# Re-costed transposes and selects in a list scheduler that orders a fused attention and two-mixture kernel

## The chip, the cores and the metric

One core of a Trainium2 chip runs the whole program in one launch. The metric is device time in microseconds, from the program's start to its end on that core. The profiled execution gives, beside its own time, the span from its first to its last instruction.

The engines are TensorE (PE in the rows; PEld is its weight loads), VectorE (DVE), ScalarE (ACT), GpSimd (POOL) and SyncE (SP, which here issues every DMA and every DMA transpose).

## The reference

```python
scores = scale * np.matmul(q, k.transpose(0, 1, 3, 2))
cum = np.cumsum(np.log(np.clip(f, 0.0001, 1.0)), axis=-1)
decay = cum[:, :, :, None] - cum[:, :, None, :]
scores = np.where(causal, -1000000000.0, scores + decay)
attn = softmax(scores)                       # over the last axis
x = np.matmul(attn, v)                       # 4 batches, 8 heads, 576 rows, head size 64
x = x.transpose(0, 2, 1, 3).reshape(2304, 512)
h = x @ w_in                                 # 512 -> 2048
x = np.maximum(0.01 * h, h) @ w_out          # 2048 -> 512
g = x @ w_gate                               # 512 -> 1536
out = (silu(g) * (x @ w_val)) @ w_out2       # 1536 -> 512
```

Everything is float32 outside; the weights arrive as 64-bit words from which the kernel assembles float32 by integer operations.

## The kernel before, in words

**Precision.** Most products run as three half-precision products of a high and a low half (TERMS = high x high, high x low, low x high). `split` makes the two halves: ScalarE writes the high half, VectorE the low one from it.

**Units of work.** Each batch is cut into two units of queries, the first of 320 (three tiles of 128, the first half empty) and the second of 256 (two tiles). For a unit, `attention` goes through four pairs of heads. For every head it loads queries and keys (`in_qk_dram`), makes TensorE's score products, lets VectorE add the causal mask and take the row extreme (the custom instruction that writes `att_bytes` from a bank), lets ScalarE take the exponential, and `probs` writes the two halves of the normalised probabilities into one tile. A DMA transpose on SyncE turns that tile: 12 blocks of 128 x 128 two-byte numbers in a first unit, 18 in a second one. There are 56 of these. `pv` (a product of transposed probabilities and values) then fills the rows of one pair, and a ScalarE and a VectorE instruction write its high and low half into `xs_buf`, which lies in `moe_bytes`. The first unit of the first batch goes another way, in float32, with diagonal matrices that GpSimd makes by `affine_select` (line 858).

**The mixture behind.** While the attention of one unit runs, TensorE gets the first mixture of the unit before as filling: `moe_h` (banks from `moe_bytes` and `wi_bytes`) and `moe_y` (banks from `g_bytes` and `wo_bytes`). So at the end of every unit there is a handover: the last `pv` of the unit, its two halves, and then the first `moe_h` group, which reads them. Between them VectorE also assembles the next weights from words (tiles `stage`, `wi_bytes`, `wo_bytes`) and stores them for later. After the last unit the second mixture runs alone, on TensorE above all, to the end.

**What sets the order.** No instruction is issued when its function is called. `Plan.record` keeps it with a reckoned duration from `cost` (line 149 on), `link` finds what depends on what, and `emit` (line 382) searches an order. `schedule` is a list scheduler over five queues: at each step the engine that is free first takes the ready piece that is due earliest. `backward` sets new due times from the far end, and the next round uses them. This is done in rounds, for two lead times of loads. `trial` then reckons each order's end under several cases of random lateness of the DMAs, and the order with the smallest sum is issued, in program order on each engine. On the chip every engine works through its own queue strictly in that order and waits by semaphores where a piece's input is not there. The reckoned durations are thus in the order only; they are no part of the program.

In the first 18 us, and where the plan has TensorE pause early on, `emit` puts warming matmuls on a spare bank (line 412).

Since all instructions are issued from line 415, rows are told apart by tiles, not by lines.

## Time and profile before

| | us |
|---|---|
| median of 3 runs | 925.02 |
| lowest and highest | 922.46, 925.94 |
| the profiled execution, its own time | 925.66 |
| its span, first to last instruction | 923.9 |

The profile's rows say how long an engine was busy, how long one instruction took on average, and in brackets how long the engine stood before it and who ended that. A waiting engine costs time only if it is on the way to the end.

### The profile page before, as it was taken

The page shows a single profiled execution, that of the slowest core. Times are in us where ns is not written, and L with a number is a line of the kernel's source. Part 1 is how long each engine was busy: PE and PEld are TensorE (multiplying, and loading weights), DVE is VectorE, ACT ScalarE, POOL GpSimd, SP SyncE. Part 2 cuts the span into 40 slices and gives each one's busy share as a digit, 9 for nine tenths or more (in the row PEclk, how much of TensorE's full clock was granted, in tenths as well). Part 3 has the DMA queues.
Part 4 walks back from the last instruction along what each step waited for, and adds up shares of the span by engine and source line. Part 5 has one row for each costly group of instructions (what it writes and reads, how often), then busy time and mean ns, then how long its engine had stood idle before and what let it go on. Part 6 is the DMA issues. An engine that isn't in the chain of part 4 may idle for free.

```text
span 923.9 us, 25387 instructions
## 1 busy us (share of the span) xinstructions
PE 908.8 (98%) x10018; PEld 776.7 (84%) x10018; DVE 794.1 (86%) x2078; ACT 676.1 (73%) x1665; POOL 45.4 (5%) x119
## 2 busy tenths in 40 slices
PE   9999999999999999899999999999999999999998
PEld 5666678877688777788778899999999999999997
DVE  7999999988899999799788999986778695968685
ACT  8886689988689887688886878774647474755553
POOL 3410000000000010000000000000000000000000
PEclk9999999999999999999999999999999999999999
DMA  7568985797999999989867452110101000100001
GB/s 229 179 202 217 271 212 115 187 248 172 259 270 259 255 263 229 298 249 254 188 147 191 140 178 96 64 59 20 37 18 31 25 25 25 37 25 2 26 6 42
DMA packets 163431, 132.81 MB, mean 144 GB/s; under 512 B 117432, under 2 KB 130752, under 8 KB 163280
## 3 DMA queue, kind: packets, MB, share of 16 engines
q1 hardware_dynamic: 163312, 131.20, 53.5%
q8 instruction: 78, 1.28, 0.6%
q14 instruction: 41, 0.34, 0.1%
HBM read 79.99 MB, written 22.83 MB: 111 GB/s over the span
## 4 chain that ended last, share of the span: by engine, by line
PE 58%; DVE 7%; DMA 3%; ACT 3%; issue 1%; POOL 0%; SPq 0%; ACTq 0%; DVEq 0%; POOLq 0%
PE bank L415 58%; DVE att_bytes L415 2%; DVE stage L415 1%; DVE wo_bytes L415 1%; ACT att_bytes L415 1%; DMA tb<-out_dram 1%; ACT moe_bytes L415 1%; DMA att_bytes<-att_bytes 1%; DVE smalls L415 1%; DVE wi_bytes L415 1%; DMA att_bytes<-in_qk_dram 1%; DMA gate_val_dram<-wo_bytes 1%; DVE g_bytes L415 1%; DVE tb L415 0%; DVE ta L415 0%
## 5 line engine op out<-in xcount | busy, mean ns | idle before, releaser
L415 PEld LDWEIGHTS <-att_bytes 128*128 128x128 f16 (+1 forms) x4062 | 233.8, 100 | 18.3 <-issue 14.7
L415 PEld LDWEIGHTS <-wi_bytes 128*128 128x128 f16 x2292 | 192.2, 98 | 42.4 <-issue 3.1
L415 PE MATMUL bank<-g_bytes,wo_bytes 128*128 128x256 f16 (+2 forms) x1472 | 209.7, 299 | 0.0
L415 PE MATMUL bank<-moe_bytes,wi_bytes 128*128 128x320 f16 (+1 forms) x1536 | 194.5, 286 | 1.5 <-ACT moe_bytes L415 1.5
L415 ACT ACTIVATE att_bytes<-att_bytes,smalls 128x320 f32<-128x320 f32 (+11 forms) x308 | 173.7, 591 | 30.1 <-DVE smalls L415 25.5
L415 PEld LDWEIGHTS <-wo_bytes 128*128 128x128 f16 x1344 | 128.1, 98 | 33.5 <-issue 1.8
L415 DVE TENSOR_TENSOR wi_bytes<-bank,wi_bytes 128x256 f32<-128x256 f32 x270 | 109.4, 418 | 45.0 <-PE bank L415 43.6
L415 PEld LDWEIGHTS <-g_bytes 128*128 128x128 f16 x1620 | 125.9, 98 | 9.0
L415 ACT ACTIVATE wi_bytes<-wi_bytes,smalls 128x256 f32<-128x256 f32 (+2 forms) x129 | 69.9, 555 | 44.9 <-DVE wi_bytes L415 42.4
L415 PE MATMUL bank<-wi_bytes,att_bytes 128*128 128x128 f16 x1680 | 98.7, 219 | 0.5 <-ACT wi_bytes L415 0.3
L415 DVE SCALAR_TENSOR_TENSOR att_bytes<-att_bytes,smalls 128x576 f16<-128x576 f32 (+5 forms) x148 | 86.8, 614 | 4.1 <-ACT att_bytes L415 3.7
L415 PE MATMUL bank<-stage,att_bytes 128*128 128x128 f16 (+1 forms) x1389 | 86.7, 221 | 0.6 <-DVE wi_bytes L415 0.6
L415 ACT COPY wi_bytes<-bank 128x256 f32<-128x256 f32 x108 | 38.4, 363 | 51.8 <-PE bank L415 47.6
L415 DVE CUSTOM_DVE_ANT_0 att_bytes<-bank,att_bytes 128x320 f32<-128x320 f32 (+5 forms) x160 | 67.7, 441 | 7.2 <-PE bank L415 7.1
L415 POOL PARTITION_ALL_REDUCE smalls<-smalls x54 | 28.2, 523 | 757.1 <-DVE smalls L415 718.3
L415 PE MATMUL bank<-att_bytes 128*64 128x256 f16 (+4 forms) x828 | 55.5, 262 | 5.5 <-DMA att_bytes<-att_bytes 5.2
L415 ACT ACTIVATE wi_bytes<-wo_bytes 128x256 bf16<-128x256 f32 x108 | 44.0, 410 | 19.2 <-DVE wo_bytes L415 19.2
L415 PE MATMUL bank<-wo_bytes,g_bytes 128*128 128x256 f16 x432 | 55.0, 273 | 0.0
L415 DVE TENSOR_TENSOR g_bytes<-moe_bytes,g_bytes 128x320 f16<-128x320 f32 (+1 forms) x80 | 44.6, 564 | 8.2 <-ACT g_bytes L415 7.8
L415 PE MATMUL bank<-tb 68*128 68x256 f32 (+3 forms) x144 | 49.9, 360 | 1.7 <-ACT att_bytes L415 1.1
L415 DVE SCALAR_TENSOR_TENSOR stage<-stage 128x512 int32<-128x512 int32 x68 | 46.5, 684 | 0.2
L415 DVE SCALAR_TENSOR_TENSOR wo_bytes<-wi_bytes,smalls 128x512 f32<-128x512 f32 x54 | 40.1, 743 | 6.3 <-ACT wi_bytes L415 6.3
(123 smaller groups left out, 1380.1 us busy)
## 6 DMA issues: line engine op xcount, KB each, us to landing
stage<-in_moe_w_out_dram SPq DMA_DIRECT2D x28, 512.0 KB
att_bytes<-in_qk_dram SPq DMA_DIRECT2D x24, 416.0 KB
stage<-in_moe_w_in_dram SPq DMA_DIRECT2D x16, 512.0 KB
att_bytes<-in_qk_dram SPq DMA_DIRECT2D x24, 320.0 KB
stage<-in_moe_w_gate_dram SPq DMA_DIRECT2D x12, 512.0 KB
stage<-in_moe_w_val_dram SPq DMA_DIRECT2D x12, 512.0 KB
stage<-gate_val_dram SPq DMA_DIRECT2D x12, 512.0 KB
ta<-y_dram SPq DMA_DIRECT2D x18, 256.0 KB
```

What stands on the lines that cost most here:

```text
L415: fn(*args, **kw)
```

## The change

Four numbers of the scheduler's reckoning and the size of its search:

```diff
--- before.py
+++ after.py
@@ -160,7 +160,7 @@
         if eng == "SP":
             k = n(o) * o.shape[0] * mybir.dt.size(o.dtype)
             if method == "dma_start_transpose":
-                return 18.5 * k / 4096, k
+                return 24.4 * k / 4096, k
             return 510.0, k
         m = max(n(x) for x in outs + ins)
         psum = any(x.space == PSUM for x in ins)
@@ -172,7 +172,7 @@
                 return 374.0, 0
             if method == "memset":
                 return 0.83 * m + 48, 0
-            return (4.2 if ptrs else 0.75 if method == "affine_select" else 2.104) * m + 148, 0
+            return (4.2 if ptrs else (3.04 if ins[0].dtype == F32 else 0.75) if method == "affine_select" else 2.104) * m + 148, 0
         if method == "reciprocal":
             return 6.4 * m + 69, 0
         if method == "memset":
@@ -304,7 +304,7 @@
                 d += min(d, max(0.0, COLD - t) / 2)
             free[e] = t + d
             if e == "SP":
-                dma = max(dma, t + 500.0) + op.bytes / (260.0 if op.dur > 1e3 else 280.0)
+                dma = max(dma, t + 500.0) + op.bytes / (210.0 if op.dur > 1e3 else 280.0)
                 op.end = max(dma + 1200.0 + self.MARGIN, t + self.flight(op))
             else:
                 op.end = t + d
@@ -366,7 +366,7 @@
             d = op.dur
             if e == "SP":
                 free[e] = t + d
-                dma = max(dma, t + 500.0) + op.bytes / (260.0 if d > 1e3 else 280.0)
+                dma = max(dma, t + 500.0) + op.bytes / (210.0 if d > 1e3 else 280.0)
                 end[op.idx] = max(dma + 1200.0, t + self.flight(op) - self.MARGIN) + lag[op.idx]
                 continue
             if e == "PE":
@@ -379,7 +379,7 @@
             free[e] = end[op.idx] = t + d
         return max(end)
 
-    def emit(self, rounds=40, trials=4):
+    def emit(self, rounds=60, trials=6):
         self.link()
         bank = self.filler[0].tensor.name
         lags = []
```

`k` is a transpose's bytes, so the first number is nanoseconds per 4,096 bytes that a transpose holds SyncE's queue. The 210 and 260 are bytes per nanosecond in the queue of transfers, for transposes alone (only they are reckoned above 1,000 ns on SyncE). The 3.04 is nanoseconds per column of a float `affine_select` without per-row pointers. With 60 rounds and two lead times 120 orders are made, and each is tried in six cases.

No instruction changes; there are two more warming matmuls (46 in place of 44), and the others stand in another order. On TensorE 398 of the 1,402 scheduled pieces stand elsewhere, on VectorE 1,210 of 1,886, on ScalarE 748 of 1,308, on SyncE 235 of 423, on GpSimd 29 of 115. TensorE's last 653 pieces, VectorE's last 458 and ScalarE's last 332 stand as before.

SyncE's queue at the end of the attention of batch 2, second unit: the last two transposes of the unit, before:

```order
L415 DMA tb_87<-cum_dram 4x640
L415 DMA att_bytes<-in_v_dram 128x640
L415 DMA_TRANSPOSE att_bytes<-att_bytes 128x18x128
L415 DMA stage<-in_moe_w_out_dram 128x1024
L415 DMA att_bytes<-in_qk_dram 128x640
L415 DMA out_dram<-wi_bytes 128x512
L415 DMA att_bytes<-in_qk_dram 128x640
L415 DMA_TRANSPOSE att_bytes<-att_bytes 128x18x128
```

and now:

```order
L415 DMA tb_87<-cum_dram 4x640
L415 DMA att_bytes<-in_v_dram 128x640
L415 DMA_TRANSPOSE att_bytes<-att_bytes 128x18x128
L415 DMA out_dram<-wo_bytes 128x512
L415 DMA stage<-in_moe_w_out_dram 128x1024
L415 DMA att_bytes<-in_qk_dram 128x640
L415 DMA_TRANSPOSE att_bytes<-att_bytes 128x18x128
L415 DMA out_sums_dram<-stage 128x1024
```

A store (`out_dram<-wo_bytes`) and a load (`stage<-in_moe_w_out_dram`) that followed the second transpose now stand between the two, and a load and a store that stood between them now stand ahead of the first.

VectorE at the handover behind batch 0's second unit. The row that writes `moe_bytes` 128x256 is the low half which the next `moe_h` reads; `bank_70` and `bank_71` are score banks, `wo_bytes<-wo_bytes` are low halves of weights. Before:

```order
L415 ISA att_bytes,smalls<-bank_71,att_bytes 128x320
L415 ISA smalls 128x1
L415 TENSOR_SCALAR smalls<-smalls 128x3
L415 RECIPROCAL smalls<-smalls 128x1
L415 TENSOR_TENSOR ta_85<-att_bytes,ta_85 64x320
L415 RECIPROCAL smalls<-smalls 128x3
L415 TENSOR_TENSOR tb_87<-att_bytes,ta_85 64x320
L415 SCALAR_TENSOR_TENSOR wo_bytes<-wo_bytes,smalls 128x512
L415 SCALAR_TENSOR_TENSOR moe_bytes<-bank_72,smalls,moe_bytes 128x256
L415 TENSOR_REDUCE smalls<-att_bytes 128x1
```

and now:

```order
L415 TENSOR_SCALAR smalls<-smalls 128x1
L415 RECIPROCAL smalls<-smalls 128x1
L415 RECIPROCAL smalls<-smalls 128x3
L415 TENSOR_SCALAR smalls<-smalls 128x1 x2
L415 RECIPROCAL smalls<-smalls 128x1
L415 SCALAR_TENSOR_TENSOR wo_bytes<-wo_bytes,smalls 128x512
L415 TENSOR_SCALAR smalls<-smalls 128x3
L415 RECIPROCAL smalls<-smalls 128x3
L415 TENSOR_TENSOR ta_85<-att_bytes,ta_85 64x320
L415 TENSOR_TENSOR tb_87<-att_bytes,ta_85 64x320
L415 SCALAR_TENSOR_TENSOR wo_bytes<-wo_bytes,smalls 128x512
L415 SCALAR_TENSOR_TENSOR moe_bytes<-bank_72,smalls,moe_bytes 128x256
```

Ten instructions that followed the low half now stand ahead of it (one reduction and one weight half of them just above the piece shown); 4.04 us by their own durations in the trace.

VectorE at the handover behind batch 3's first unit, from the last score reduction of that stretch (`bank_71`, 128x288) to the low half (`moe_bytes`, 128x320). Before:

```order
L415 ISA att_bytes,smalls<-bank_71,att_bytes,smalls 128x288
L415 ISA smalls 128x1
L415 SCALAR_TENSOR_TENSOR att_bytes<-att_bytes,smalls 128x448
L415 TENSOR_SCALAR stage<-stage 128x512
L415 SCALAR_TENSOR_TENSOR stage<-stage 128x512
L415 TENSOR_SCALAR smalls<-smalls 128x2
L415 SCALAR_TENSOR_TENSOR moe_bytes<-bank_72,smalls,moe_bytes 128x320
L415 RECIPROCAL smalls<-smalls 128x2
```

and now:

```order
L415 ISA att_bytes,smalls<-bank_71,att_bytes,smalls 128x288
L415 ISA smalls 128x1
L415 RECIPROCAL smalls<-smalls 128x2
L415 SCALAR_TENSOR_TENSOR stage<-stage 128x512
L415 SCALAR_TENSOR_TENSOR wo_bytes<-stage 128x512
L415 SCALAR_TENSOR_TENSOR att_bytes<-att_bytes,smalls 128x576
L415 SCALAR_TENSOR_TENSOR att_bytes<-att_bytes,smalls 128x448
L415 TENSOR_SCALAR smalls<-smalls 128x2
L415 RECIPROCAL smalls<-smalls 128x2
L415 TENSOR_TENSOR tb_87<-att_bytes,ta_85 64x576
L415 SCALAR_TENSOR_TENSOR att_bytes<-att_bytes,smalls 128x576
L415 SCALAR_TENSOR_TENSOR moe_bytes<-bank_72,smalls,moe_bytes 128x320
```

Four instructions stood between the reduction and the low half (the second row writes the reduction's result out); now nine do. Three low halves of probabilities are among them (`att_bytes<-att_bytes,smalls`), a score operand (`tb_87`), two weight assemblies, and the small steps that end in the second reciprocal.

## Rows read from the trace of the kernel before

**Rows 1.** The page's head and busy times by engine.

```profile
span 923.9 us, 25387 instructions
...
PE 908.8 (98%) x10018; PEld 776.7 (84%) x10018; DVE 794.1 (86%) x2078; ACT 676.1 (73%) x1665; POOL 45.4 (5%) x119
```

**Rows 2.** Stretches: bounds and length, busy us by engine, clock, DMA share, GB/s.

```profile
125.00:150.00 25.00, 25.00 (x233) 21.42 (x232) 23.01 (x71) 24.23 (x59) 2.01 (x9) 1.00 0.70 158
350.00:400.00 50.00, 47.65 (x437) 38.57 (x434) 43.53 (x125) 37.77 (x92) 1.30 (x7) 0.97 1.01 268
400.00:450.00 50.00, 48.74 (x446) 40.28 (x446) 48.47 (x145) 44.69 (x116) 0.30 (x2) 1.00 1.00 247
600.00:650.00 50.00, 50.00 (x710) 47.74 (x708) 38.54 (x83) 29.29 (x74) 1.34 (x2) 1.00 0.13 40
```

**Rows 3.** Who waited for whom: total us, times, longest us.

```profile
PE bank L415 <- DMA att_bytes<-att_bytes: 5.2, 3, 2.3
...
PE bank L415 <- ACT moe_bytes L415: 1.5, 3, 0.7
...
PE bank L415 <- ACT att_bytes L415: 1.1, 1, 1.1
```

**Rows 4.** A stretch of TensorE alone: busy us, clock, DMA share, GB/s.

```profile
375.00:385.00 10.00, 10.00 (x89) 0.83 1.00 299
```

**Rows 5.** Timeline near 250 us, SyncE and TensorE: start, us, instruction [idle before, releaser].

```profile
244.99 1.64 SPq L415 DMA_DIRECT2D y_dram<-moe_bytes  x1
...
247.22 3.29 SPq L415 DMA_TRANSPOSE att_bytes<-att_bytes  x1
...
252.31 1.56 PE L415 MATMUL bank<-att_bytes 128*64 128x256 f16 x29 [1.62 <-DMA att_bytes<-att_bytes]
...
254.69 0.50 PE L415 MATMUL bank<-moe_bytes,wi_bytes 128*128 128x256 f16 x3
```

**Rows 6.** Timeline near 110 us, SyncE and TensorE.

```profile
102.15 5.50 SPq L415 DMA_TRANSPOSE att_bytes<-att_bytes  x1
...
110.64 1.53 PE L415 MATMUL bank<-att_bytes 128*64 128x256 f16 x28 [1.26 <-DMA att_bytes<-att_bytes]
```

**Rows 7.** Timeline near 370 us, all engines, some rows left out.

```profile
367.68 4.80 SPq L415 DMA_TRANSPOSE att_bytes<-att_bytes  x1
367.74 0.68 ACT L415 ACTIVATE stage<-wo_bytes 128x512 f32<-128x512 f32 x1 [2.50 <-DVE wo_bytes L415]
...
374.68 1.79 PE L415 MATMUL bank<-att_bytes 128*64 128x256 f16 x29 [2.35 <-DMA att_bytes<-att_bytes]
...
376.40 3.19 PE L415 MATMUL bank<-g_bytes,wo_bytes 128*128 128x320 f16 x12
```

**Rows 8.** SyncE's transposes: count, ns min/median/max, first and last start.

```profile
L415 SPq DMA_TRANSPOSE att_bytes<-att_bytes x56: 1279/3174/7080, 79.0 to 486.9; - x56
```

**Rows 9.** Groups on GpSimd: count, busy us, mean ns, idle before and releasers.

```profile
L415 POOL TENSOR_SCALAR_AFFINE_SELECT g_bytes<-smalls 128x128 f32<-128x128 f32 x24 | 11.5, 506 | 19.6 <-DVE smalls L415 16.8 <-PE bank L412 1.4 <-PE bank L415 1.4
```

**Rows 10.** Groups on TensorE: the warming matmuls.

```profile
L412 PE MATMUL bank<-att_bytes 128*128 128x512 bf16 x44 | 14.0, 456 | 1.6 <-POOL att_bytes L415 1.6
```

**Rows 11.** Timeline near 132 us: VectorE's low half, TensorE's matmuls that read it.

```profile
132.60 0.47 DVE L415 SCALAR_TENSOR_TENSOR moe_bytes<-bank,smalls,moe_bytes 128x256 f16<-128x256 f32 x1
...
132.68 4.54 PE L415 MATMUL bank<-moe_bytes,wi_bytes 128*128 128x256 f16 x40
```

**Rows 12.** Timeline near 434 us: VectorE, ScalarE's high half, TensorE's matmuls that read it.

```profile
431.63 0.17 DVE L415 RECIPROCAL smalls<-smalls 128x2 f32<-128x2 f32 x1
...
433.51 0.51 DVE L415 CUSTOM_DVE_ANT_0 att_bytes<-bank,att_bytes,smalls 128x288 f32<-128x288 f32 x1
...
435.19 0.51 ACT L415 ACTIVATE moe_bytes<-bank,smalls 128x320 f16<-128x320 f32 x1
...
435.75 4.45 PE L415 MATMUL bank<-moe_bytes,wi_bytes 128*128 128x320 f16 x31 [0.71 <-ACT moe_bytes L415]
...
436.24 0.15 DVE L415 RECIPROCAL smalls<-smalls 128x2 f32<-128x2 f32 x1
```

## The prediction

> **What bounds the kernel now.** I read the busy shares first, then who waited for whom, then stretches, then short timelines. TensorE is busy for 908.8 of 923.9 us [rows 1]. So a better order can win only the time in which TensorE pauses, about 15 us, and part of that is the start and the last microseconds. The matmuls stay the same whatever the order.
>
> The second thing to see is that VectorE (DVE) is almost as full in the first half and not in the second: 23.01 of 25 us busy at 125 to 150, 43.53 of 50 at 350 to 400, 48.47 of 50 at 400 to 450, but 38.54 of 50 at 600 to 650 [rows 2]. The two engines are in balance up to about 550 us; behind that TensorE alone decides. And behind that the new order is nearly the old one: of TensorE's 1,402 scheduled pieces the last 653 stand exactly where they stood, as do VectorE's last 458 (the two programs' orders tell this). Everything below therefore plays before about 575 us.
>
> The table of waits names the pauses that the changed numbers are about: TensorE waited three times for a transpose, 5.2 us in all, 2.3 us at most [rows 3]. The last one was costlier than it looks. In the stretch from 375 to 385 us the granted clock averages 0.83 [rows 4]: after the 2.35 us pause TensorE ran at the lower of its two levels for about 10 x (1 - 0.83) / 0.5 = 3.4 us and so lost another 1.7 us. Behind the 1.62 us pause at 252 us [rows 5] the matmuls kept their speed.
>
> **What the new numbers say, against the trace.** A large transpose (18 blocks, 589,824 bytes by its shape) was reckoned to hold SyncE 144 x 18.5 ns = 2.66 us, and is now reckoned at 144 x 24.4 ns = 3.51 us. The three before the pauses held it 5.50, 3.29 and 4.80 us [rows 6, 5, 7], so the new number is nearer. A small one (12 blocks) goes from 1.78 to 2.34 us, while the shortest of all 56 took 1.28 us [rows 8]; for these it moves away from the shortest. A select on a float tile goes from 244 to 537 ns, and the mean is 506 [rows 9]. So two of the three corrections are right. None of them changes an instruction's real cost; they change only the order. The larger search (60 rounds and six cases in place of 40 and four) costs the chip nothing.
>
> On the rate: 589,824 bytes used 252.31 - 247.22 = 5.09 us after issue is 116 GB/s from issue to use [rows 5], and that includes latency, so the trace alone does not tell 260 from 210. The Trainium skill (DMA: Bandwidth & Descriptors, section Latency and other measured facts) gives 261 GB/s for a transpose with a strided middle dimension, close to the old figure and against the new one. By that page the new order would allow 2,809 - 2,260 ns = 0.55 us too much for each large transpose, an estimate, and the slower rival below would gain weight.
>
> **The change part by part.** I use durations of the rows and count what stands ahead of what in the two orders.
>
> 1. Start: 46 warming matmuls instead of 44. The 44 keep TensorE 14.0 us [rows 10], 0.32 us each: **+0.6 us** if both lie on the path, nothing if they fill a real pause. The selects' new order moves GpSimd's instructions by three places at most; I set that at nothing, as GpSimd's 24 selects are 11.5 us in all [rows 9] and lie beside VectorE work.
>
> 2. The product of attention and values at 110 us waits 1.26 us for a transpose issued at 102.15 [rows 6]. In the new order VectorE's last step before that transpose stands where it was, and TensorE has 0.64 us more matmuls ahead of the product (by the same matmuls' spacing in the trace): **-0.6 us**.
>
> 3. The same at 250 us, 1.62 us [rows 5]. The transpose went out at 247.22 because SyncE stood behind a store that held it 1.64 us and was issued ahead of it. The new order puts that store behind the transpose, and three score products ahead of the waiting product; in the trace they lie between its end, 252.31 + 1.56, and 254.69, some 0.8 us. 1.64 + 0.8 is more than 1.62: **-1.6 us**.
>
> 4. The same at 372 us, 2.35 us [rows 7]. Here TensorE gets 2.65 us more ahead of the product (three score products, 1.0 us by their spacing, and one group of 12 matmuls, which at the lower clock took 3.19 us and at the upper one about half). Against that, a load and a store that followed the transpose in SyncE's queue now stand ahead of it. The load needs a buffer whose last reader, ScalarE's 0.68 us step, started at 367.74, so the transpose cannot go before about 368.5 + 2 x 0.4 = 369.3, that is 1.6 us later. The pause shrinks by 2.65 - 1.6 = 1.05 to 1.3 us. That is shorter than the 1.62 after which the clock stayed up, so the 1.7 us go as well: **-2.7 us**. Bounds: 0 and -4.05.
>
> 5. Handover at 130 us, from the last product of one unit to the first hidden-layer matmuls of the mixture that consumes it. ScalarE writes the high half, VectorE the low half (start 132.60, 0.47 us), and the matmuls need the low half four matmuls after 132.68, at 133.1 [rows 11]. It was just in time. In the new order 4.04 us of other VectorE work is moved ahead of it, ten instructions that overlap by some 0.07 us each, so 3.4 us (the order shown above has them). If VectorE is no earlier at that place than now, TensorE pauses 3.4 us; if it has found all of it in gaps, nothing. With 23.01 of 25 us busy I take the upper part: **+2.5 us**.
>
> 6. Handover at 434 us [rows 12]. TensorE stands 0.71 us for the high half. In the new order ScalarE makes that half behind another probability step, and this needs a reciprocal that VectorE does only after seven instructions behind its last score reduction (the first is the 0.17 us reciprocal, the last the 0.15 us one; all seven 3.35 us, less overlap 2.9). From the reduction's end at 434.02 this gives 436.9, then 0.78 and 0.51 us on ScalarE with a step of 0.1 between: 438.3, against 435.7 now, **0 to +2.6 us**. VectorE has 6.5 us of idle time at 350 to 400 [rows 2], which work moved ahead can fill, so I take **+1.5 us**, without a fall of the clock.
>
> Handovers at 186, 254, 308 and 378 us show the same pattern, 1.2 to 6.6 us of VectorE work moved ahead; TensorE gets up to 1 us more there and, at 378, ScalarE and VectorE stood idle for over a microsecond each. I set them at nothing; at the upper end they are in the slower rival.
>
> Sum: 0.6 - 0.6 - 1.6 - 2.7 + 2.5 + 1.5 = **-0.3 us**. The profiled execution took 925.66 us, so 925.4; it lies 0.6 us above the median of 925.02. On the median's footing I say **924.7 us**.
>
> **The rivals.**
> *Faster: the moved work finds real gaps.* If VectorE does the work moved ahead while it would have idled, points 5 and 6 cost nothing, and the sum is -4.3 us. If TensorE's waits for ScalarE go too, 1.5 and 1.1 us [rows 3], it is -6.9: 918.1 us. For it: two of three corrections fit the rows. Against it: VectorE's idle time before 130 us is small.
> *Slower: the handovers pause longer than 2.35 us.* Both late halves then also bring the clock down, as the 2.35 us pause did. Its price is 3.4 + 1.7 at 130 us and 2.6 + 1.7 at 434; with 0.6 at the start, -0.6 and -1.6 from points 2 and 3 and nothing from point 4, that is +7.8: 932.8 us; with a microsecond at each of two more handovers, 934.8. It decides once a half lands more than 2.35 us behind the matmul that needs it. For it: the moved work is in the same direction at every handover. Against it: a pause early in the half makes TensorE late for all that follows and hides later ones.
> *The change does nothing that counts:* the order moves but pauses only change places, since TensorE is full and the later half the same. That gives 925.0, give or take 2, inside my forecast.
>
> **How the numbers follow.** A run of this kernel can tell about 0.5%, 4.6 us, from no change. I give the forecast (with the third rival, some 0.15 of it) 0.50, the faster rival 0.25, the slower 0.25. The range reaches to both rivals' ends, 918 to 935. The forecast's own range is 920.5 to 929.5.
>
> **What would show it.** Right: the wait for transposes falls from 5.2 to about 2 us; no stretch near 375 us has a clock under 1.00; TensorE newly waits 1 to 3 us for VectorE or ScalarE near 133 and 436 us; TensorE's busy time beyond 600 us is unchanged. Wrong: handovers without a pause (then the faster rival), or stretches near 133 or 436 us with a clock under 1.00 (the slower one), or a transpose wait that is as long elsewhere.

## The result and the profile after the change

The change takes 928.97 us (median of 7 runs, 927.92 to 932.79) against 922.46 us for the kernel before (7 runs, 921.74 to 925.94). The ratio is 1.0067, with a 95% interval of 1.0047 to 1.0088: **0.67% slower**, 6.5 us. I had forecast no change (924.7 us) and given slower a chance of one in four. The time lies inside the range, but that is partly luck: the base of the forecast, 925.02 us from three runs, was itself 2.6 us above the later median of before.

The profiled execution took 929.61 us. The page's head, as in [rows 1]:

```profile
span 927.9 us, 25394 instructions
...
PE 909.1 (98%) x10016; PEld 778.5 (84%) x10020; DVE 794.3 (86%) x2078; ACT 677.3 (73%) x1665; POOL 48.4 (5%) x119
```

TensorE, VectorE and ScalarE have hardly more to do. TensorE is busy for 909.1 us as against 908.8, and the span is 4.0 us longer; the difference is TensorE standing still. Who it waited for, as in [rows 3] (total us, times, longest):

```profile
PE bank L415 <- ACT moe_bytes L415: 5.6, 4, 2.4
PE bank L415 <- DMA att_bytes<-att_bytes: 3.4, 2, 2.9
...
PE bank L415 <- DVE wi_bytes L415: 1.6, 3, 0.9
PE bank L415 <- DVE smalls L415: 1.5, 3, 0.7
```

The waits for transposes fell from 5.2 to 3.4 us, but the longest grew from 2.3 to 2.9. The waits for `moe_bytes`, the high halves at the handovers, rose from 1.5 to 5.6 us. The stretches, as in [rows 2, 4] (bounds and length, busy us of PE, PEld, DVE, ACT, POOL, clock, DMA share, GB/s):

```profile
125.00:150.00 25.00, 22.11 (x194) 18.86 (x194) 23.56 (x69) 24.73 (x61) 1.89 (x5) 0.93 0.67 149
131.00:141.00 10.00, 9.85 (x90) 9.00 (x90) 9.47 (x24) 10.00 (x25) 0.32 (x3) 0.83 0.58 149
350.00:400.00 50.00, 47.86 (x446) 38.64 (x444) 46.26 (x137) 38.78 (x95) 1.68 (x8) 1.00 1.04 280
400.00:450.00 50.00, 47.03 (x420) 38.44 (x418) 47.26 (x143) 42.73 (x108) 0.66 (x3) 0.97 0.95 256
436.00:446.00 10.00, 8.21 (x47) 5.26 (x47) 9.46 (x26) 8.13 (x20) 0.00 (x0) 0.83 0.93 217
```

The lower clock that stood at 375 to 385 us in the profiled execution of before is gone (1.00 over 350 to 400). It stands behind 131 and behind 436 us instead, each time 10 x (1 - 0.83) / 0.5 = 3.4 us at 1.2 instead of 2.4 GHz, which costs half of that.

**The handover near 131 us**, timeline (start, us, instruction [idle before, releaser]):

```profile
122.19 0.88 DVE L415 SCALAR_TENSOR_TENSOR att_bytes<-att_bytes,smalls 128x640 f16<-128x640 f32 x1
123.15 1.32 DVE L415 SCALAR_TENSOR_TENSOR att_bytes<-att_bytes,smalls 128x576 f16<-128x576 f32 x2
124.53 3.27 SPq L415 DMA_TRANSPOSE att_bytes<-att_bytes  x1
127.97 0.30 PE L415 MATMUL bank<-att_bytes 128*64 128x256 f16 x1
131.15 2.24 PE L415 MATMUL bank<-att_bytes 128*64 128x256 f16 x29 [2.89 <-DMA att_bytes<-att_bytes]
```

The unit's last product (x1, then x29) starts one matmul at 127.97 and stands 2.89 us for the transpose that SyncE issued at 124.53. That issue came right behind VectorE's two low halves of 576 columns (end 124.47), and ahead of these the change put a low half of 640 columns. But before, the same transpose went out hardly earlier, as SyncE was still held by the one ahead of it, and its product didn't wait:

```profile
124.29 2.74 SPq L415 DMA_TRANSPOSE att_bytes<-att_bytes  x1
...
129.73 1.59 PE L415 MATMUL bank<-att_bytes 128*64 128x256 f16 x30
```

In old_again (below) the issue came at 124.62, later than now, and there was no wait either. So two other things changed. TensorE comes 1.76 us earlier (127.97 against 129.73). And the transpose takes longer: of the 16 signals by which the trace shows it done, the last came 4.6 us after the issue before (128.87) and 6.6 us after it now (131.11). The DMA view of 116 to 133 us, in 40 slices of 0.425 us, shows a stop inside it (7, 5 and 10 GB/s, from 128.75 to 130.03):

```profile
GB/s 288 416 277 136 255 239 173 288 201 139 229 345 230 273 267 237 234 121 139 265 349 386 302 257 134 34 201 214 240 196 7 5 10 212 411 277 390 377 380 386
```

Why it stopped isn't shown.

**The handover near 437 us**, as in [rows 12]:

```profile
436.01 0.17 DVE L415 RECIPROCAL smalls<-smalls 128x2 f32<-128x2 f32 x1
...
436.35 0.78 ACT L415 ACTIVATE att_bytes<-att_bytes,smalls 128x576 f16<-128x576 f32 x1
437.03 0.51 ACT L415 ACTIVATE moe_bytes<-bank,smalls 128x320 f16<-128x320 f32 x1
...
437.59 0.70 PE L415 MATMUL bank<-moe_bytes,wi_bytes 128*128 128x320 f16 x4 [2.37 <-ACT moe_bytes L415]
```

ScalarE writes the high half at 437.03 instead of 435.19, behind a probability step (436.35) that needs the reciprocal at 436.01. TensorE stands 2.37 us instead of 0.71.

### The profile page after: what moved, and what is told of

Read it like the earlier page. It is cut to its first block, busy times and chain, and to the rows that moved or that the text cites. A ratio compares the mean times of both kernels' runs of the same rounds, so it can differ in the third digit from the quotient of the medians.

```text
span 927.9 us, 25394 instructions
## 1 busy us (share of the span) xinstructions
PE 909.1 (98%) x10016; PEld 778.5 (84%) x10020; DVE 794.3 (86%) x2078; ACT 677.3 (73%) x1665; POOL 48.4 (5%) x119
## 4 chain that ended last, share of the span: by engine, by line
PE 74%; DVE 16%; DMA 3%; issue 3%; ACT 2%; POOL 1%; POOLq 0%; DVEq 0%; ACTq 0%
PE bank L415 73%; DVE att_bytes L415 5%; DVE wi_bytes L415 3%; DVE stage L415 3%; DVE smalls L415 1%; DMA att_bytes<-att_bytes 1%; DVE wo_bytes L415 1%; ACT att_bytes L415 1%; DMA stage<-in_moe_w_out_dram 1%; PE bank L412 1%; DVE moe_bytes L415 1%; DVE tb L415 1%; DVE ta L415 1%; POOL smalls L415 1%; DMA g_bytes<-out_sums_dram 1%
## 5 line engine op out<-in xcount | busy, mean ns | idle before, releaser
L415 ACT ACTIVATE att_bytes<-att_bytes,smalls 128x448 f16<-128x448 f32 (+11 forms) x308 | 173.1, 589 | 28.0 <-DVE smalls L415 21.9
L415 DVE SCALAR_TENSOR_TENSOR att_bytes<-att_bytes,smalls 128x320 f16<-128x320 f32 (+5 forms) x148 | 86.6, 613 | 3.3 <-ACT att_bytes L415 3.1
L415 POOL PARTITION_ALL_REDUCE smalls<-smalls x54 | 31.1, 575 | 736.0 <-DVE smalls L415 733.5
L415 PE MATMUL bank<-att_bytes 128*64 128x256 f16 (+3 forms) x828 | 56.0, 263 | 4.3 <-DMA att_bytes<-att_bytes 3.4
L415 ACT ACTIVATE moe_bytes<-bank 128x320 f32<-128x320 f32 (+1 forms) x80 | 39.1, 492 | 14.4 <-PE bank L415 14.3
```

The lines of the kernel that those rows point to most:

```text
L415: fn(*args, **kw)
```

## The experiments

Two theories stood against each other. The first: the loss is made at two handovers, and each pause also brings the clock down. The second: lateness at one place is only shifted from others, so mending a place wins nothing. To place gains and losses I compare when two executions reach the same amount of TensorE's matmuls (at equal matmuls, for short).

Where an experiment has an order of its own, the scheduler's search is replaced by a written list of the recorded pieces. OLD is the order of before, NEW that of the change; numbers are pieces. Ratios are to before, whose median over these runs was 923.3 to 924.2 us; 0.1% is 0.92 us.

### The kernel before once more, and the change in thirds

**old_again** has no edit. 

> The kernel before once more, for a second trace of it. Its profiled execution took 925.66 us against a median of 922.46. If the pause of 2.35 us near 374 us and the fall of the clock behind it belong to every execution, they are here again. If they belong to the slower executions alone, this one takes about 922 us, the pause is under 2 us and the clock stays up, and point 4 of the prediction removed something that the median never paid.

It took 922.78 us, near the median of before. Behind a pause of 1.99 us at 373 us its clock stayed up (the stretch that is 0.83 in [rows 4]):

```profile
375.00:385.00 10.00, 10.00 (x90) 8.70 (x89) 8.93 (x28) 8.36 (x25) 0.00 (x0) 1.00 1.02 305
```

So the execution on which I worked (925.66 us) was 3.2 us above the later median, and the clock fall that I meant to win back isn't in every execution: of the 94 runs of before beside these experiments, 49 have a mean clock of 0.998 or less, which one fall of 3.4 us makes, and 45 have more. The pause at 252 us is shorter here too, 0.66 us instead of 1.62. How late the two others are against this one, at equal matmuls:

| at (us) | 116 | 137 | 197 | 338 | 400 | 420 | 441 | 623 |
|---|---|---|---|---|---|---|---|---|
| first profile of before | +0.6 | -0.2 | +0.2 | +1.0 | +2.8 | +2.3 | +2.3 | +2.9 |
| the change | -1.9 | +2.2 | +1.8 | +1.6 | +2.5 | +2.7 | +6.1 | +6.4 |

The change is ahead until 116 us, loses 4.0 us up to 137 and 3.4 between 420 and 441. Everything else together is 0.9. One execution differs from another by up to 2 us in this measure: middle_new below has before's order up to 205 us and is 1.9 us ahead of old_again at 197.

**first_new**, **middle_new**, **last_new**: the change's order up to 205 us, from 205 to 413 us, and from 413 us, the rest as before.

```diff
-    order = NEW
+    order = OLD[:1250]
+    for part in (NEW[:2450], OLD):
+        order += [i for i in part if i not in set(order)]
```

(That is middle_new, with the bounds written in; first_new is NEW[:1250] and then OLD, last_new OLD[:2450] and then NEW.)

> The new order up to about 205 us (where both orders have issued the same pieces), the old one behind it. Theory: the loss is made at two handovers, at 131 us (2.89 us pause and a fall of the clock, +4.6 us by the trace) and at 437 us (+3.4). Then this kernel has the first alone: it leaves the first part 1.6 us late by the trace of the change, and the old order's later pauses may hide some of that: 0 to +2.5 us against the kernel before. Rival: the loss is spread over many small waits, then all three parts lose about 2 us each.

> The new order from about 205 to 413 us alone. Theory: -2 to +0.5 us against the kernel before, as the trace of the change gains 2 us there and no clock falls. Rival (spread loss): +2 us.

> The old order up to about 413 us, the new one behind it. Theory: the late high half at 437 us and the fall of the clock cost +3 to +4 us against the kernel before, nearly all in the stretch 430 to 450 us. Rival (spread loss): +2 us, with no fall of the clock.

| | median us | ratio | interval |
|---|---|---|---|
| first_new | 926.60 | 1.0034 | 1.0021 to 1.0047 |
| middle_new | 921.84 | 0.9979 | 0.9967 to 0.9991 |
| last_new | 933.43 | 1.0103 | 1.0086 to 1.0120 |

In first_new the lower clock is back in the stretch near 131 us:

```profile
125.00:150.00 25.00, 21.66 (x193) 18.87 (x194) 23.45 (x71) 23.93 (x58) 1.90 (x6) 0.93 0.66 159
```

By the medians the middle third gains 0.2% and the first costs 0.3%. The traces don't show where the middle gains: between 197 and 420 us middle_new loses 1.3 us on old_again at equal matmuls, and its lead at the end was won where its order is before's. Last_new has a pause of 2.38 us at 440 us for the high half, but also two pauses (2.15 and 1.47 us) at 415 to 417 us which the change doesn't have; these are made by the cut. So its size says nothing.

### The two handovers, mended singly and together

**half_ahead**: at 433 us the two halves go ahead.

```diff
+    order = [i for i in order if i not in (2543, 2544, 2606, 2659)]
+    k = order.index(2542) + 1
+    order[k:k] = [2606, 2543, 2544, 2659]
```

> The change's order with one edit near 433 us: ScalarE writes the high half of the unit's last product ahead of the two steps (an exponential of the decay and a probability step) that the change put before it, and VectorE the low half ahead of three of its steps. Nothing else moves. Theory (the 2.37 us pause at 437.6 us is this half standing behind the probability step, and the clock fall of 3.41 us is the pause's): the high half is written by about 434.7 us, the pause falls to 0.7 us or less as in [rows 12], the clock stays at 1.00 there, and the time falls by 1.7 + 1.7 = about 3.4 us against the change, to about 925.5. Rival (VectorE and TensorE are late there for other reasons, the half only shows it): a pause of over 1.5 us stays within 5 us behind that place, for another wait, and the time falls by under 1 us.

927.07 us, ratio 1.0036 (1.0024 to 1.0049) against the change's 1.0067: 0.31%, 2.9 us, regained (the two intervals just touch). The pause and the stretch:

```profile
436.64 2.24 PE L932 MATMUL bank<-moe_bytes,wi_bytes 128*128 128x320 f16 x15 [0.53 <-ACT moe_bytes L932]
```

```profile
376.00:386.00 10.00, 8.29 (x72) 6.50 (x67) 9.91 (x31) 8.45 (x22) 0.00 (x0) 0.83 0.98 273
436.00:446.00 10.00, 9.22 (x67) 6.43 (x66) 9.66 (x27) 9.32 (x23) 0.00 (x0) 1.00 1.05 223
```

Between 420 and 441 us it loses 0.2 us where the change lost 3.4. In this execution the clock fell at 380 us, behind pauses of 1.42 and 0.29 us. The theory holds at this place.

**loads_behind**: at 125 us two loads go behind the transpose.

```diff
+    order = [i for i in order if i not in (941, 711, 712, 713, 714, 715, 984, 716)]
+    k = order.index(769) + 1
+    order[k:k] = [941, 711]
+    k = order.index(783) + 1
+    order[k:k] = [712, 713, 714, 715, 984, 716]
```

> The change's order with one edit near 125 us: on SyncE the query/key load and the value load, which the change put directly ahead of the last transpose of the unit, go behind it again (as before), and the five VectorE steps and one GpSimd step that use the value load go behind the unit's last low half. Nothing else moves. Theory (the pause of 2.89 us at 131 us is the transpose landing late, 6.62 us after its issue, because the data of two 320 KB loads go ahead of it on the DMA engines): issue stays at about 124.5 us (it waits for VectorE), landing comes 5.4 us or less behind it, at 129.9 us or earlier, the pause is 1.7 us or less, the clock stays at 1.00 behind it, and the time falls by 1.2 + 1.7 = about 3 us against the change, to about 926. Rival (TensorE is simply 1.8 us earlier at that place than before, and the transpose is as late as its own issue makes it): landing stays near 131.1 us, the pause near 2.9 us, the clock falls, and the time is that of the change.

930.90 us, 1.0081 (1.0063 to 1.0100). The pause is still 2.53 us:

```profile
130.63 1.56 PE L934 MATMUL bank<-att_bytes 128*64 128x256 f16 x29 [2.53 <-DMA att_bytes<-att_bytes]
```

The DMA view of 116 to 134 us, in 40 slices of 0.45 us:

```profile
GB/s 329 285 200 230 225 201 265 134 97 242 341 216 283 290 283 162 0 0 0 0 0 148 213 212 217 214 208 220 131 387 347 381 297 225 273 387 378 381 245 157
```

From 123 to 125 us the DMA engines move nothing. Bandwidth was not short; the transpose simply wasn't issued, as SyncE waited for the low halves. The pause and the time are nearer to the rival, but the theory of the loads is not settled by this. The transpose went out at 124.37, and 15 of its 16 signals came by 129.00, 4.6 us later, earlier than the theory asked (129.9); the last came at 130.59. With it in time the pause would have been about 0.9 us (an estimate: 129.00 less 128.10, the end of the x1). The clock, too, stayed up behind this pause, and in both_edits behind one just as long.

A late end of this transpose stands behind every pause of over 2 us at this place. In half_ahead, both_edits, only_hold and only_rate, too, the last signal came 1.5 to 1.7 us behind the fifteenth; in the change and in first_new all 16 came late together. From issue to last signal these seven took 6.1 to 6.6 us. In before, old_again, low_ahead and first_mended it took 4.6 to 4.8, and TensorE didn't wait for it.

At equal matmuls loads_behind loses 2.7 us from 116 to 137 us, where the change lost 4.0, but 2.0 more from there to 197: TensorE stood 1.66 us at 174 us for nothing that the profile shows, which the change did not.

**both_edits** is both diffs. 

> Both edits, that of the loads near 125 us and that of the half near 433 us, in the change's order. Theory (the two places are the whole of the change's cost, and each costs its pause and 1.7 us of lower clock): the gains add, about -6.4 us against the change, to about 922.5, on a level with the kernel before or 1 to 2 us below it; no stretch of half clock behind 20 us. Rival (lateness won at 131 us is lost again at a later wait, as VectorE is the bound in between): under 4 us against the change.

927.87 us, 1.0056 (1.0035 to 1.0076): no gain over half_ahead. What it won up to 137 us it lost again by 197, with the same standstill at 174 us (1.68).

**low_ahead**: loads_behind, and the 640-column low half with its small steps goes behind the two low halves of the transpose.

```diff
+    late = [941, 659, 792, 793, 794, 795, 796, 711, 712, 713, 714, 715, 984, 716]
+    order = [i for i in order if i not in late]
+    k = order.index(769) + 1
+    order[k:k] = late[:8]
+    k = order.index(783) + 1
+    order[k:k] = late[8:]
```

> The change's order with the two low halves of which the unit's last transpose is made put ahead again, as before: on VectorE a 128x640 low half, three small steps on row sums and one more (1.5 us in all, 0.30 us of it a wait for GpSimd), which the change put before them, go behind them, and with them the query/key load and the value load on SyncE as in the run loads_behind. Theory (the product at 131 us waits because the change moved 1.5 us of VectorE work ahead of the two low halves, so that the transpose could not be issued before 124.3 to 124.5 us, while TensorE came 1.8 us earlier): the two low halves end near 123 us, the transpose is issued there, lands about 6.3 us later as in loads_behind, near 129.3 us, and the pause falls from 2.5 to 2.9 us to about 1.3 us; without a clock fall. Against the change -1.4 - 1.7 = about -3 us, 926. Rival (SyncE or the DMA engines are the limit, as the transpose before it holds SyncE until 122.5 and the data go one after the other): landing stays within 0.5 us of 130.6, the pause above 2 us.

930.72 us, 1.0080 (1.0063 to 1.0097). No gain, but a telling timeline (rows of SyncE, ScalarE, VectorE and TensorE):

```profile
123.55 2.69 SPq L935 DMA_TRANSPOSE att_bytes<-att_bytes  x1
...
128.65 1.59 PE L935 MATMUL bank<-att_bytes 128*64 128x256 f16 x30
...
133.03 0.73 ACT L935 ACTIVATE wo_bytes<-wo_bytes,smalls 128x512 f16<-128x512 f32 x1
133.65 0.56 ACT L935 ACTIVATE att_bytes<-att_bytes,smalls 128x320 f16<-128x320 f32 x1
134.10 0.47 ACT L935 ACTIVATE moe_bytes<-bank,smalls 128x256 f16<-128x256 f32 x1
...
134.62 0.79 PE L935 MATMUL bank<-moe_bytes,wi_bytes 128*128 128x256 f16 x3 [2.79 <-ACT moe_bytes L935]
```

The transpose goes out 0.8 us earlier than in loads_behind, all its signals are there at 128.11, and the product (x30) doesn't wait. Then the matmuls behind it stand 2.79 us for the high half, which ScalarE writes only at 134.10, behind a weight-scaling step (`wo_bytes`) and a probability step. **Two late things lay behind each other here; the first had hidden the second.**

**first_mended**: low_ahead, and six weight-scaling steps go behind the halves as well.

```diff
+    late = [802, 803, 804, 805, 806, 807]
+    order = [i for i in order if i not in late]
+    k = order.index(783) + 1
+    order[k:k] = late
```

> The order of low_ahead (in which the wait for the transpose at 131 us was gone, and a pause of 2.79 us for the unit's last high half stood at 134.6 us in its place), with the six steps of ScalarE and VectorE that scale weights (three each, tile wo_bytes, 0.61 to 0.75 us each) put behind the unit's last two halves again, as before. Theory (two late things lie one behind the other at this handover, the transpose and the halves; either hides the other, and the change brought both by the work it moved ahead): no pause above 0.7 us from 125 to 140 us beside a standstill of TensorE's own issue, no clock fall there, and about 4 us less than the change, 925; beside low_ahead 5 to 6 less. Rival (TensorE is early there, and a third thing holds it): a pause of over 2 us remains between 125 and 140 us.

935.31 us, 1.0124 (1.0107 to 1.0141). At the place itself the theory held: a standstill of TensorE's issue (`issue`: it waited for nothing that the profile shows), then a pause of 0.71 us, the clock at 1.00.

```profile
127.01 0.39 PE L939 MATMUL bank<-tb 68*128 68x320 f32 x1 [1.20 <-issue]
...
133.70 8.50 PE L939 MATMUL bank<-moe_bytes,wi_bytes 128*128 128x256 f16 x75 [0.71 <-ACT moe_bytes L939]
```

But the work put behind was due. From 140 to 180 us TensorE now waits 3.2 us for VectorE and ScalarE (and 1.7 for nothing shown):

```profile
PE bank L939 <- issue: 1.7, 1, 1.7
PE bank L939 <- ACT moe_bytes L939: 1.2, 1, 1.2
PE bank L939 <- DVE smalls L939: 1.0, 3, 0.6
PE bank L939 <- DVE g_bytes L939: 0.7, 2, 0.5
PE bank L939 <- ACT g_bytes L939: 0.3, 1, 0.3
```

At equal matmuls it loses 2.1 us from 116 to 137 us instead of 4.0, and then 6.4 up to 197, of which these rows show 4.9.

At 131 us, then, the second theory fits better: moving single pieces won nothing. ScalarE and VectorE are nearly full there ([rows 2], 24.23 and 23.01 of 25 us); that this is the reason was not tried by itself. Of the written orders those that reached before's time have its first third (middle_new, middle_halves).

**change_mended**: NEW with the diffs of low_ahead and half_ahead and, at the handovers at 251, 306 and 376 us, the halves put ahead by the diff of middle_halves below. **all_mended**: the same with first_mended for low_ahead.

> The change's order with all mends at once: the two low halves ahead near 123 us (low_ahead), the high and low half ahead near 433 us (half_ahead), and at 251, 306 and 376 us (as in middle_halves). Theory (these places are the whole of the change's cost): -3 at 131 us, -3.3 at 437 us, -2 to -2.5 at the three others, against 928.97: 920 to 921, below the kernel before; no stretch of half clock behind 20 us. Rival (lateness moves on to the next wait): above 924.

> The order of change_mended (halves ahead at 251, 306, 376 and 433 us) with the mend of first_mended at 131 us in place of low_ahead's. Theory (the handovers are the whole of the change's cost, and the removed waits at 110, 250 and 372 us its gain): change_mended's 926.75 less 4.5 (its pause of 2.85 us at 136 us and the 1.7 us behind it), about 922, on a level with before or up to 2 us below it. Rival (VectorE's and ScalarE's work put behind the halves makes up for it elsewhere before 205 us): above 925.

926.75 us, 1.0039 (1.0024 to 1.0054), and 931.23 us, 1.0080 (1.0061 to 1.0099). Neither reaches before. Change_mended still pauses 2.85 us at 136 us. The rival, lateness that moves on, is right in the first third.

**warmed**: the change's order with TensorE kept at work through both pauses.

```diff
+WARM = {781: [(12, 3)], 2558: [(10, 6)]}
...
+            for n, bank in WARM.get(i, ()):
+                ps, w, x = self.filler
+                for _ in range(n):
+                    self.tensor.real.matmul(self.banks[bank], lhsT=w, rhs=x, start=True, stop=True)
```

> The change's order, with warming matmuls (products whose result nobody reads) on the bank that the waiting product writes next: 12 ahead of the product that waits at 131 us, 10 ahead of the hidden-layer group that waits at 437 us, about 2.6 and 2.2 us at the upper clock. The waits themselves stay. Theory (each fall of the clock is an effect of the pause before it and costs 3.41 us at half speed, 1.7 us of work): no stretch of half clock at 131 or 437 us, the bare pauses under 0.5 us, the time 2 x 1.7 = 3.4 us below the change, about 925.5. Rival (the lower clock comes from something else in that stretch, or TensorE's lateness there is made good behind it anyway): the time stays within 1 us of the change.

928.20 us, 1.0047 (1.0029 to 1.0064). The clock stays up in both stretches:

```profile
125.00:150.00 25.00, 24.20 (x215) 19.49 (x215) 23.58 (x72) 24.64 (x60) 2.21 (x8) 1.00 0.71 163
430.00:450.00 20.00, 18.65 (x147) 13.40 (x147) 18.52 (x53) 17.39 (x40) 0.92 (x2) 1.00 1.04 261
```

The mean clock is 1.00 in seven of the nine runs, while all seven of the change lie between 0.992 and 0.998. So at these places the clock fell because TensorE stood still. What that cost is not settled: the time is 0.2% less than the change's, between the two expectations, with overlapping intervals. At equal matmuls the places cost 3.0 and 2.5 us instead of 4.0 and 3.4, 1.9 us less together, where I had reckoned 3.4.

### Which of the four edits

Each run is the kernel before with one edit of the diff: 24.4 alone, 210 alone (both places), the select's 3.04 alone, and the larger search alone.

> The kernel before with one of the change's edits: the transposes' hold of SyncE at 24.4 in place of 18.5 ns per row of blocks; the scheduler then finds an order of its own. In it the 128x640 low half is not ahead of the two low halves near 123 us, and the last high half of the unit near 433 us stands behind another step, not behind the one that it stood behind in the change. Theory (the time follows from those two places, and the hold is the correction that the trace bears out): no pause above 2 us at 131 or 437 us, 920 to 925. Rival (any new order of this scheduler loses some microseconds, whatever number is changed): 926 or more.

> The kernel before with one of the change's edits: 210 in place of 260 bytes per ns for a transpose; the scheduler finds an order of its own. In it one of the two low halves near 123 us comes 0.6 us later than the other, the value load stands ahead of the unit's last transpose as in the change, and the last high half near 433 us does not stand behind the probability step that it stood behind in the change. If the rate is the number that brings the value load and late transposes at 131 us: a pause of over 2 us there and none at 437 us, 924 to 928. If each order loses and wins by chance: anywhere between 920 and 930, with the pauses at other places.

> The kernel before with one of the change's edits: selects on float tiles at 3.04 in place of 0.75 ns an element, 537 in place of 244 ns each; the scheduler finds an order of its own. GpSimd does 24 of these in 11.5 us and waits are put down to it only at the start. If orders cost by what they correct, this one gives nothing: 922 to 925. If any new order loses some microseconds, as only_hold did (926.60 beside 924.21): 926 or more.

> The kernel before with one of the change's edits: 60 rounds and six cases in place of 40 and four, the costs as they were. The order it takes stands near before's: 459 of TensorE's instructions, 564 of VectorE's and 246 of ScalarE's differ by place. At 131 us nothing differs; the last high half near 433 us stands behind two probability steps as before. If each new order loses whatever brought it: 926 or more. If the loss comes from the new numbers, which put far more in other places: within 2 us of before, 922 to 926.

| | median us | ratio | interval |
|---|---|---|---|
| only_hold | 926.60 | 1.0022 | 1.0007 to 1.0037 |
| only_rate | 928.44 | 1.0044 | 1.0028 to 1.0060 |
| only_select | 937.18 | 1.0150 | 1.0127 to 1.0174 |
| only_search | 924.48 | 1.0004 | 0.9994 to 1.0013 |

The larger search does nothing: alone it stays within 0.1%, and with the three new numbers the smaller search issues the same program. Each new number alone makes the kernel slower, the select most, though it corrects GpSimd instructions that TensorE hardly waits for. It does so at other places; only_select's waits:

```profile
PE bank L415 <- DMA att_bytes<-att_bytes: 6.6, 4, 3.0
PE bank L415 <- DVE moe_bytes L415: 5.1, 4, 1.7
PE bank L415 <- DVE smalls L415: 2.7, 4, 1.5
```

Only_rate comes nearest to the change: 2.42 us for the transpose at 133 us, and the clock falls there. Only_hold, whose 640-column low half is not ahead, still pauses 2.24 us for the transpose at 133 us, against the theory that I had written for it. Each of the three new numbers sends the search to another order, and all three lost; the larger search gave another order too and lost nothing. Why the search prefers these orders was not tried, nor whether any change of the numbers would lose because the old order is a lucky one.

### A version below both kernels

**middle_halves**: middle_new's order, and at its three handovers the steps that ScalarE and VectorE did ahead of the halves go behind them. **middle_halves_again** is the same kernel.

```diff
+HALVES = [(1462, [1521, 1531, 1539]), (1463, [1540, 1541]),
+          (2206, [2353, 2178, 2300]), (2207, [2355, 2356, 2180, 2301]),
+          (1833, [1823, 1824, 1881]), (1834, [1727, 1728, 1674, 1882])]
...
+    for half, late in HALVES:
+        order = [i for i in order if i not in late]
+        k = order.index(half) + 1
+        order[k:k] = late
```

> The order of the run middle_new (before's to 205 us, the change's from there to 413 us, before's again), and at the three handovers in it (near 251, 306 and 376 us) ScalarE writes the high half of the unit's last product, and VectorE the low half, ahead of two to four steps that they did in the meantime. Theory (a handover's pause is the half's place in the queue, as half_ahead showed at 437 us): the pauses of 1.45, 0.59 and 1.20 + 0.32 us fall to under 0.5 us each, and the time falls by 2 to 2.5 us against middle_new's 921.84, to about 919.5, which is below the kernel before. Rival (the work put behind the halves then makes the next product late, since both engines are almost full there): the pauses come back within 10 us, and the time is within 1 us of middle_new's.

> The kernel of the run middle_halves once more, as its profiled execution lay 3 us above its median. If its gain holds (0.9956 of before): 918.5 to 921.5 beside before's 922.5 to 924.2, and the profiled execution without a stretch of half clock behind 20 us. If it was this one chip: a ratio of 0.998 to 1.002.

919.61 us, 0.9956 (0.9938 to 0.9974), and 919.09 us, 0.9945 (0.9924 to 0.9966): **0.5% below before and about 1% below the change**. Between 197 and 420 us middle_halves_again wins 1.5 us on old_again at equal matmuls, where middle_new lost 1.3. TensorE's waits in middle_new

```profile
PE bank L932 <- ACT moe_bytes L932: 3.2, 3, 1.4
...
PE bank L932 <- DMA att_bytes<-att_bytes: 1.5, 2, 1.2
```

and in middle_halves_again:

```profile
PE bank L937 <- DMA att_bytes<-att_bytes: 1.5, 2, 1.0
...
PE bank L937 <- ACT moe_bytes L937: 0.6, 1, 0.6
```

## Why the prediction was wrong, point by point

**The steps that failed** are the terms at the handovers and the waits that I took as won. Points 5 and 6 stood at +4.0 us and measured +7.4, each with a fall of the clock that the sum had at nothing. Points 3 and 4 stood at -4.3 and measured +0.5 (the table from 137 to 420 us): the pauses were longer in the one execution that I read than in the next, and other waits, set at nothing, took their place.

1. *Start, +0.6.* Not seen. The change is 0.1 us ahead at 54 us.
2. *110 us, -0.6.* Right in kind: the pause is gone. By 116 us the change is 1.9 us ahead.
3. *250 us, -1.6.* The wait for the transpose is gone, but a pause of 1.47 us for the high half follows at 256 us. The step that failed is that of the other handovers, "I set them at nothing"; the gain comes to 0.3 us (245 to 262 us). The 1.62 us were no standing cost either: in old_again it is 0.66.
4. *372 us, -2.7.* The pause for the transpose is gone and the clock stays up, as I said. Two errors ate it: pauses of 0.71 us for a small step and 1.19 + 0.24 for the handover took its place, and the 1.7 us of clock were no standing cost, as old_again and about half of the runs of before show. Against old_again the change loses 0.9 us between 338 and 400.
5. *130 us, +2.5.* Measured +4.0. The step that failed: my term knows one thing that TensorE can wait for here, VectorE's low half. The transpose that the unit's last product needs is not in it, and this was the wait, 2.89 us: TensorE came 1.76 us earlier than before (I had 0.64 in point 2), and the transpose was done 6.6 us after its issue instead of 4.6. The 640-column low half is not the reason, as the issue moved by only 0.24 us; why the transpose took longer stays open. A late half was there as well, behind it, but ScalarE's high half: the 2.79 us in low_ahead, inside my 0 to 3.4. The clock fall came on top.
6. *434 us, +1.5.* The mechanism is as I worked it out, and the size is off: measured +3.4, of which 1.66 us are a longer pause and half of 3.41 us the clock. The clause "without a fall of the clock" is the term that was mis-sized. ScalarE had the half written at 437.54; my latest was 438.3.

The sum of my terms was -0.3, that of the steps in the table is +6.4. The **slower rival** was nearest: it had +7.8, with both pauses over 2.35 us and both falls of the clock, and 6.5 was measured. At 131 us it is right by luck in part, as it has a late half there and the pause was the transpose's. I gave it 0.25, with the reason against it that an early pause hides later ones; the one at 131 us did not hide the one at 437. Points 2 to 4 were certain only as to the wait that they removed.

On the rate, the trace differs from the page that I cited (the Trainium skill, DMA: Bandwidth & Descriptors, Latency and other measured facts, 261 GB/s). In loads_behind a transpose has the DMA engines to itself from 126 to 128.6 us and moves 208 to 220 GB/s. The new figure of 210 is the better one, and the order made with it is slower all the same.

## What to carry to other kernels

Better costs in a list scheduler don't give a better order by themselves. What counted at 437 us and in middle_halves is what stands ahead of the few instructions that a full engine waits for, so look there in the new order, at every handover. When you cost a removed wait, list everything else that the same consumer needs and when it is ready: the next latest thing is what you get. And before you count a pause or a fall of the clock as a gain, see in a second execution whether it is there each time. When a transfer is late, compare its issue with that of the kernel before: here it was the same, and an order of instructions that seemed to explain the lateness did not.

## What the chip showed that was not expected

- Falls of the clock don't follow the length of the pause alone. They came behind 2.35, 2.89, 2.37 and 2.79 us, but also at 380 us in half_ahead behind 1.42 and 0.29, and at 373 us in middle_halves behind 0.74 and 0.70. None came behind 3.02 us in only_select (259 us), 2.53 in loads_behind and 1.99 in old_again. In middle_halves_again pauses of 0.76 and 0.70 us stand at the same place without a fall. Each of these falls lasted 3.41 us; one in last_new, behind 2.15 and 1.47, lasted 6.83.
- TensorE stood 1.2 us at 126 to 127 us (low_ahead, first_mended) and 1.7 us at 174 us (loads_behind, both_edits) for nothing that the profile shows. What it was stays open.
- At 131 us the same transpose of 18 blocks took 4.6 us from issue to last signal in some orders and 6.1 to 6.6 in others: one of the 16 signals came 1.6 us late or, in the change, the data stopped for 1.3 us. What held them stays open.
